# w_in in two halves behind the third v, the last unit's second layer by columns, and a new order table

## The chip, the cores and the metric

The kernel runs on one core of one Trainium2 chip. A time is device microseconds (us) of one execution, and the kernel's time is the median over executions. Each of the core's engines works off its own instructions strictly in their order: TensorE (PE) multiplies matrices, VectorE (DVE) and ScalarE (ACT) work elementwise and can read PSUM, where TensorE's results stand, GpSimd (POOL) works elementwise in SBUF, and SyncE (SP) issues DMAs. Here GpSimd issues DMAs as well, those of the weights. An instruction that waits holds up everything behind it on its engine, whatever that is.

## The reference

A gated linear attention gives x, and a two-layer network with a leaky relu is applied to x. Per batch and head, with f = sigmoid(f_logit):

```python
for t in range(S):
    state = f[:, :, t, :, None] * state + np.einsum('bhd,bhe->bhde', k[:, :, t], v[:, :, t])
    y[:, :, t] = np.einsum('bhd,bhde->bhe', q[:, :, t], state)
...
x = y.transpose(0, 2, 1, 3).reshape(B * S, H * D)
h = x @ w_in
g = np.maximum(0.01 * h, h)
out = g @ w_out
```

B = 4, H = 8, S = 768, D = 48, so x is 3072 x 384; w_in is 384 x 2048 and w_out 2048 x 384. All inputs and the output are float32.

## The kernel before, in words

The sequence is cut into 6 chunks of 128 steps. A pair j (0 to 11) is one chunk of two batches, c = j // 2 and h = j % 2; a unit (j, a) with a = 0 or 1 is one chunk of one batch, 128 rows of x. Attention goes unit by unit: a cumulative sum of log-gates by a matmul with a triangle of ones, q and k scaled with its exponentials and transposed, scores masked by the triangle, and a state of 48 x 48 per head carried from chunk to chunk. The first layer takes 16 blocks of 128 columns of w_in, the second 16 blocks of rows of w_out.

The tile framework's own scheduling is switched off. What runs when is a table of words written out by hand (`order`, L320 to L378). A loop (L379 to L381) takes word after word and records the instructions of that step, each on its engine; so the table fixes every engine's order, and semaphores fix the rest. A word is a step, the pair j, the unit a, and for some steps a third number:

- `Lf`, `Lk`, `Lq`, `Lv`: SP loads one unit's f_logit, k, q or v, 192 KB (L96 to L99); six buffers each. `st`: SP stores one unit's output (L303).
- `gate`, `dec`: ACT makes the log-gates and the exponentials. From pair 6 on, `gate`, `k`, `q` and `v` take both units in one instruction. `k`, `q`: the scaling (L155 to L165), on VectorE for k of pairs 0 to 5 and q of pairs 0 to 2, else on GpSimd. `v`: GpSimd casts v (L167 to L174).
- TensorE: `cs` (cumulative sum), `tk`, `tq` (transposes, which VectorE copies out in `ck`, `cq`), `sc` (scores, masked by VectorE in `mk`), `mx` (output of the attention, copied out by VectorE in `xt`), `pt` (state update from k and the cast v, L245 to L249; VectorE adds it in `sf`, GpSimd decays and casts the state in `sb`).
- First layer: `uu_j_a_g` (L281), four blocks of columns, 512 of w_in's 2048, for one unit, 12 matmuls, in pairs 0 to 3; `up_j_g` (L268), two blocks for both units, 6 matmuls. ACT applies the leaky relu in `pu` and `pr`. Their results stand in two PSUM buffers (`ps_m`), so a third first-layer step waits for the relu of the first.
- Second layer: `dn_j_a_quarter` (L293), four matmuls of 384 columns; four quarters make one unit, accumulated in one of two PSUM buffers (`ps_o`), which VectorE copies out in `ob` (L299).
- `W_piece_x_j_a` (L104): GpSimd issues DMAs of weights. Pieces 0 to 2 are columns of w_in (L102), three DMAs each; pieces 3 to 6 are quarters of w_out, one DMA each. The first word with a given (x, j, a) first copies one element of that unit's f, k, q or v (x = 0 to 3) to `gate_w` (L108), so the DMAs are issued only when that load has landed.
- `H_piece` (L122): SP reads four elements of that w_in piece, so what stands behind it in SP's queue is issued only when the piece has landed.

Raw loads, weight pieces and stores share the core's 16 DMA engines. SP's queue holds loads and stores in the order of the table: a store that waits for its copy holds up the loads behind it.

Of the kernel before, what the change touches and what calls it, by code (L numbers as in the profile page):

```python
# [9 lines left out]
FP32 = mybir.dt.float32  # L10
# [5 lines left out]
def kernel(  # L16
# [85 lines left out]
    w_in_cols = ((0, FF // 4), (FF // 4, FF // 2), (FF // 2, FF))  # L102
# [200 lines left out]
    def store(j, a):  # L303
        c, h = pairs[j]
        t = (2 * h + a) * S + c * C
        nc.sync.dma_start(out=out[t:t + C, :], in_=st[j].pop(("osb", a)))
# [7 lines left out]
        "up": up, "pr": relu, "uu": up_unit, "pu": relu_unit, "W": weights, "H": hold, "dn": down, "ob": out_copy, "st": store,  # L314
        "Lf": lambda j, a: load(j, "f", a), "Lk": lambda j, a: load(j, "k", a),
# [17 lines left out]
    dec_3_0 tk_2_1 uu_2_0_2 ck_2_1 pt_2_1 pu_2_0_1 k_3_0 q_3_0 sc_2_1 pu_2_0_2 Lq_3_1 uu_2_0_3 mk_2_1_1 sf_2_1
    dn_0_1_0 pu_2_0_3 mk_2_1_0 dn_0_0_0 v_3_0 tq_3_0 mx_2_1 cq_3_0 tk_3_0 xt_2_1 sb_2_1 dn_0_0_1 ck_3_0 dn_0_1_1
    sc_3_0 uu_2_1_0 mk_3_0_0 dn_0_1_2 mk_3_0_1 pu_2_1_0 Lv_3_1 dn_0_0_2 mx_3_0 Lf_4_0 uu_2_1_1 gate_3_1 xt_3_0 Lk_4_0
    dn_0_0_3 pu_2_1_1 cs_3_1 ob_0_0 uu_3_0_0 Lq_4_0 dec_3_1 uu_2_1_2 st_0_0 pu_3_0_0 dn_0_1_3 k_3_1 q_3_1 pu_2_1_2
    uu_2_1_3 Lv_4_0 ob_0_1 v_3_1 gate_4_0 tq_3_1 dn_1_0_0 st_0_1 cq_3_1 pu_2_1_3 tk_3_1 dn_1_1_0 Lf_4_1 ck_3_1
    dn_1_0_1 Lk_4_1 sc_3_1 dn_1_0_2 Lq_4_1 mk_3_1_1 v_4_0 dn_1_1_1 mk_3_1_0 Lv_4_1 uu_3_0_1 mx_3_1 Lf_5_0 pu_3_0_1
    dn_1_1_2 xt_3_1 gate_4_1 Lk_5_0 uu_3_0_2 dn_1_0_3 Lq_5_0 pu_3_0_2 pt_3_0 cs_4_0 ob_1_0 dn_1_1_3 Lv_5_0 dec_4_0
    sf_3_0 v_4_1 cs_4_1 pt_3_1 ob_1_1 st_1_0 dn_2_0_0 sb_3_0 dec_4_1 sf_3_1 dn_2_1_0 st_1_1 k_4_0 dn_2_0_1 gate_5_0  # L340
    q_4_0 k_4_1 dn_2_1_1 Lf_5_1 sb_3_1 tq_4_0 Lk_5_1 dn_2_0_2 cq_4_0 tk_4_0 q_4_1 Lq_5_1 dn_2_0_3 ck_4_0 tk_4_1 v_5_0
    Lv_5_1 ob_2_0 tq_4_1 dn_2_1_2 cq_4_1 dn_3_0_0 st_2_0 ck_4_1 gate_5_1 dn_2_1_3 Lf_6_0 sc_4_2 ob_2_1 dn_3_0_1 Lk_6_0
    mk_4_0_1 uu_3_1_0 mk_4_0_0 st_2_1 dn_3_0_2 v_5_1 mk_4_1_1 pu_3_1_0 Lq_6_0 cs_5_0 mk_4_1_0 dn_3_1_0 dec_5_0 Lv_6_0
    mx_4_2 k_5_0 q_5_0 Lf_6_1 uu_3_1_1 xt_4_0 tk_5_0 Lk_6_1 pu_3_1_1 tq_5_0 xt_4_1 cs_5_1 uu_3_0_3 ck_5_0 dec_5_1
# [67 lines left out]
```

## Time and profile before

| | us |
|---|---|
| median of 3 runs (lowest, highest) | 195.43 (194.84, 195.71) |
| the profiled execution | 195.99 |
| its span, first to last instruction | 194.2 |
| TensorE busy | 176.0, 91% of the span |
| VectorE, ScalarE, GpSimd busy | 100.2, 98.7, 77.4 |
| second layer on TensorE (L296) | 73.4, 384 matmuls |
| first layer on TensorE (L273, L286) | 52.1 and 28.0 |
| load of one unit's f, k, q or v, issue to landing (median) | 4.3 to 4.6 |
| DMA of a quarter of w_out, issue to landing (median) | 8.4 |
| store of one unit, issue to landing (median) | 3.0 |

How lines of the profile are read: the slices cut the span into 40 equal parts of 4.9 us, and a digit is the share of the slice in tenths. In a table by stage a line gives the stage in us, its length, then busy time (and count) of TensorE's matmuls, its weight loads, VectorE, ScalarE and GpSimd, the granted clock, the DMA share and GB/s. In a timeline a line has start, length, engine, source line, operation, out<-in, shape and count; the bracket is how long the engine stood idle just before and what ended that. SPq is SP's queue; the length there is how long the issue itself took. In a list of DMA issues the last number is the median from issue to landing in us.

### The profile page before, as it was taken

The page shows a single profiled execution, that of the slowest core. Times are in us where ns is not written, and L with a number is a line of the kernel's source. Part 1 is how long each engine was busy: PE and PEld are TensorE (multiplying, and loading weights), DVE is VectorE, ACT ScalarE, POOL GpSimd, SP SyncE. Part 2 cuts the span into 40 slices and gives each one's busy share as a digit, 9 for nine tenths or more (in the row PEclk, how much of TensorE's full clock was granted, in tenths as well). Part 3 has the DMA queues.
Part 4 walks back from the last instruction along what each step waited for, and adds up shares of the span by engine and source line. Part 5 has one row for each costly group of instructions (what it writes and reads, how often), then busy time and mean ns, then how long its engine had stood idle before and what let it go on. Part 6 is the DMA issues. An engine that isn't in the chain of part 4 may idle for free.

```text
span 194.2 us, 5607 instructions
## 1 busy us (share of the span) xinstructions
PE 176.0 (91%) x2344; PEld 137.9 (71%) x2344; DVE 100.2 (52%) x211; ACT 98.7 (51%) x201; POOL 77.4 (40%) x145
## 2 busy tenths in 40 slices
PE   0566499899999999999999999999999999999992
PEld 0343389888686756888877787879788797887650
DVE  2587553388544667577544677345363666212022
ACT  4454036985381823776895765376536334443100
POOL 8228733362331571359664693407602602000000
PEclk9999999999999999999999999999999999999998
DMA  6999989899999999899999999980100200111122
GB/s 120 192 187 188 198 166 188 158 180 211 187 187 209 181 228 235 165 193 194 179 201 194 189 231 185 213 157 0 46 3 2 81 3 0 44 41 44 41 81 81
DMA packets 105201, 27.10 MB, mean 140 GB/s; under 512 B 100440, under 2 KB 104280, under 8 KB 105176
## 3 DMA queue, kind: packets, MB, share of 16 engines
q1 hardware_dynamic: 103304, 23.60, 64.2%
q0 software_dynamic: 1872, 3.15, 9.2%
q8 instruction: 18, 0.29, 0.6%
q14 instruction: 7, 0.06, 0.1%
HBM read 25.17 MB, written 4.72 MB: 154 GB/s over the span
## 4 chain that ended last, share of the span: by engine, by line
PE 80%; SPq 5%; POOL 3%; ACT 3%; DMA 2%; DVE 2%; issue 1%; POOLq 0%; DVEq 0%
PE po L296 30%; PE pm L273 22%; PE pm L286 10%; SPq L98 5%; PE py L237 5%; PE tp L185 5%; PE pw L204 4%; DMA f_raw<-in_f_logit_dram 2%; PE cs L139 2%; PE pt L248 2%; POOL qh L164 1%; ACT gT L291 1%; POOL sb L261 1%; ACT em_t L149 1%; POOL sf L258 1%
## 5 line engine op out<-in xcount | busy, mean ns | idle before, releaser
L296 PE MATMUL po<-w_out_b,gT 128*128 128x384 bf16 x384 | 73.4, 326 | 0.0
L279 ACT ACTIVATE gT<-pm 128x512 bf16<-128x512 f32 x64 | 37.7, 596 | 36.0 <-PE pm L273 35.5
L273 PE MATMUL pm<-xT,w_in_b 128*128 128x256 bf16 x384 | 52.1, 273 | 0.0
L296 PEld LDWEIGHTS <-gT 128*128 128x128 bf16 x384 | 35.7, 98 | 17.7 <-issue 0.2
L273 PEld LDWEIGHTS <-w_in_b 128*128 128x128 bf16 x384 | 40.6, 114 | 4.7 <-issue 0.2
L209 DVE TENSOR_TENSOR wm<-pw,ut 128x512 bf16<-128x512 f32 x48 | 30.6, 683 | 15.0 <-PE pw L204 14.9
L291 ACT ACTIVATE gT<-pm 128x512 bf16<-128x512 f32 x32 | 18.8, 600 | 26.7 <-PE pm L286 26.5
L301 DVE COPY osb<-po 128x384 f32<-128x384 f32 x24 | 13.3, 556 | 32.5 <-PE po L296 32.2
L286 PE MATMUL pm<-xT,w_in_b 128*128 128x128 bf16 x384 | 28.0, 228 | 0.4 <-ACT gT L291 0.3
L286 PEld LDWEIGHTS <-w_in_b 128*128 128x128 bf16 x384 | 24.6, 117 | 2.4 <-issue 0.6
L243 DVE CAST xT<-py 128x384 bf16<-128x384 f32 x24 | 12.9, 554 | 14.8 <-PE py L237 14.8
L164 POOL TENSOR_TENSOR qh<-q_raw,a_t 128x384 bf16<-128x384 f32 (+1 forms) x12 | 15.7, 1310 | 11.5 <-ACT a_end L153 9.1
L171 POOL CAST v_b<-v_raw 128x384 bf16<-128x384 f32 (+1 forms) x18 | 11.6, 642 | 21.3 <-DMA v_raw<-in_v_dram 13.7
L261 POOL CAST sb<-sf 64x192 bf16<-64x192 f32 x40 | 13.6, 341 | 13.0 <-PE py L237 10.8
L258 POOL TENSOR_TENSOR sf<-sf,a_end 128x192 f32<-128x192 f32 x20 | 10.8, 538 | 18.1 <-DVE sf L254 17.9
L133 ACT ACTIVATE e_t<-f_raw 128x384 f32<-128x384 f32 (+1 forms) x18 | 11.4, 632 | 11.5 <-DMA f_raw<-in_f_logit_dram 11.4
L158 POOL TENSOR_TENSOR kh<-k_raw,em_t 128x768 bf16<-128x768 f32 x6 | 9.9, 1647 | 13.1 <-ACT em_t L149 8.8
L149 ACT ACTIVATE em_t<-cs 128x384 bf16<-128x384 f32 x24 | 11.8, 490 | 6.2 <-PE cs L142 6.1
L139 PE MATMUL cs<-lf,ut 128*128 128x384 bf16 x24 | 8.4, 351 | 6.8 <-ACT lf L134 6.7
L188 DVE COPY qT<-tp 128x512 bf16<-128x512 bf16 x24 | 10.2, 423 | 7.0 <-PE tp L185 6.8
L188 DVE COPY kT<-tp 128x512 bf16<-128x512 bf16 x24 | 9.9, 420 | 5.4 <-PE tp L185 5.3
L185 PE MATMUL tp<-ident,qh 128*128 128x128 bf16 x96 | 10.2, 234 | 2.2 <-DVE qh L164 1.8
(44 smaller groups left out, 173.2 us busy)
## 6 DMA issues: line engine op xcount, KB each, us to landing
f_raw<-in_f_logit_dram SPq DMA_DIRECT2D x24, 192.0 KB, 4.4
k_raw<-in_k_dram SPq DMA_DIRECT2D x24, 192.0 KB, 4.5
q_raw<-in_q_dram SPq DMA_DIRECT2D x24, 192.0 KB, 4.6
v_raw<-in_v_dram SPq DMA_DIRECT2D x24, 192.0 KB, 4.3
out_dram<-osb SPq DMA_DIRECT2D x24, 192.0 KB, 3.0
w_out_b<-in_moe_w_out_dram POOLq DMA_DIRECT2D x4, 384.0 KB, 8.4
w_in_b<-in_moe_w_in_dram POOLq DMA_DIRECT2D x6, 128.0 KB, 6.5
w_in_b<-in_moe_w_in_dram POOLq DMA_DIRECT2D x3, 256.0 KB, 8.5
```

What stands on the lines that cost most here:

```text
L149: nc.scalar.activation(em[:, a], t[:, 0:H * D], AF.Exp, scale=1.0)
L164: eng.tensor_mul(qhs[j % NR][:, a, :, 0:D], raw(j, "q")[:, a], st[j]["a"][:, a].rearrange("t a (h d) -> t a h d", d=D))
L185: nc.tensor.transpose(tp[:, p, :], scaled(j, x)[:, a, 2 * p:2 * p + 2, :], ident)
L188: nc.vector.tensor_copy(out=turned(j, x)[:, P2 * a:P2 * a + P2, :], in_=st[j].pop(("tp" + x, a)))
L209: nc.vector.tensor_mul(wm, st[j].pop(("pw", a, i)), ut[:, None, :].to_broadcast([128, P2, 128]))
L261: nc.gpsimd.tensor_copy(out=sb[rows, a, :, i * D:i * D + D], in_=sf[rows, a])
L273: nc.tensor.matmul(pm[:, i, :], w_in_b[:, kk, columns(ff)], st[j]["xT"][:, kk].rearrange("t a s -> t (a s)"), start=(kk == 0), stop=(kk == ...
L279: nc.scalar.activation(gT[:, 2 * g:2 * g + 2, :], st[j].pop(("pm", g)), AF.Prelu, alpha=0.01)
L286: nc.tensor.matmul(pm[:, i, :], w_in_b[:, kk, columns(ff)], st[j]["xT"][:, kk, a, :], start=(kk == 0), stop=(kk == NK - 1))
L291: nc.scalar.activation(gT[:, 4 * g:4 * g + 4, 128 * a:128 * a + 128], st[j].pop(("pu", a, g)), AF.Prelu, alpha=0.01)
L296: nc.tensor.matmul(po, st[j]["g"][:, ff, 128 * a:128 * a + 128], w_out_b[:, ff, :], start=(ff == 0), stop=(ff == NF - 1))
L301: nc.vector.tensor_copy(out=osb, in_=st[j].pop(("po", a)))
```

## The change

w_in comes in two pieces of 1024 columns (2 x 3 DMAs) in place of pieces of 512, 512 and 1024 (3 x 3 DMAs), and GpSimd issues the first when v of unit (1,0), the third unit, has landed, not its q. SP's hold is for the first piece, which covers the same columns as before. w_out is now gated on v of unit (2,0) in place of v of (2,1). The last unit's second layer is computed by columns: first 256 columns over all 16 blocks of w_out, then 128, each part with its own PSUM buffer, copy and store (`dp`, `op`, `sp`). Six late stores are made of two DMAs of 192 columns each. The order table is new throughout: k is scaled and turned ahead of q in the first units, the steps of later units stand in other places against each other, and the last units end in another order.

The diff, with the table cut to its beginning and end:

```diff
                           in_=srcs[name][2 * h + a, :, c * C:(c + 1) * C, :].rearrange("h t d -> t h d"))
 
     seen = set()
-    w_in_cols = ((0, FF // 4), (FF // 4, FF // 2), (FF // 2, FF))
+    w_in_cols = ((0, FF // 2), (FF // 2, FF))
 
     def weights(piece, x, j, a):
 
@@ -300,10 +300,33 @@
         osb = st[j]["osb", a] = opool.tile([128, KD], FP32, name="osb", tag="osb")
         nc.vector.tensor_copy(out=osb, in_=st[j].pop(("po", a)))
 
-    def store(j, a):
+    def store(j, a, parts=1):
         c, h = pairs[j]
         t = (2 * h + a) * S + c * C
-        nc.sync.dma_start(out=out[t:t + C, :], in_=st[j].pop(("osb", a)))
+        osb = st[j].pop(("osb", a))
+        for i in range(parts):
+            cols = slice(i * KD // parts, (i + 1) * KD // parts)
+            nc.sync.dma_start(out=out[t:t + C, cols], in_=osb[:, cols])
+
+
+    last_cols = (slice(0, 256), slice(256, KD))
+
+    def down_part(j, a, i):
+        cols = last_cols[i]
+        po = st[j]["pp", i] = ps_o.tile([128, KD], FP32, name="po", tag="po")
+        for ff in range(NF):
+            nc.tensor.matmul(po[:, cols], st[j]["g"][:, ff, 128 * a:128 * a + 128], w_out_b[:, ff, cols],
+                             start=(ff == 0), stop=(ff == NF - 1))
+
+    def out_part(j, a, i):
+        cols = last_cols[i]
+        osb = once(j, ("osb", a), lambda: opool.tile([128, KD], FP32, name="osb", tag="osb"))
+        nc.vector.tensor_copy(out=osb[:, cols], in_=st[j].pop(("pp", i))[:, cols])
+
+    def store_part(j, a, i):
+        c, h = pairs[j]
+        t = (2 * h + a) * S + c * C
+        nc.sync.dma_start(out=out[t:t + C, last_cols[i]], in_=st[j]["osb", a][:, last_cols[i]])
 
     parts = {
         "gate": gate, "cs": cs, "dec": dec, "k": scale_k, "q": scale_q, "v": cast_v,
@@ -312,69 +335,70 @@
         "xk": lambda j: turn_dma(j, "k"), "xq": lambda j: turn_dma(j, "q"),
         "sc": score, "mk": mask, "mx": mix, "xt": x_out, "pt": state, "sf": state_add, "sb": state_end,
         "up": up, "pr": relu, "uu": up_unit, "pu": relu_unit, "W": weights, "H": hold, "dn": down, "ob": out_copy, "st": store,
+        "dp": down_part, "op": out_part, "sp": store_part,
         "Lf": lambda j, a: load(j, "f", a), "Lk": lambda j, a: load(j, "k", a),
         "Lq": lambda j, a: load(j, "q", a), "Lv": lambda j, a: load(j, "v", a),
     }
 
 
     order = """
-    Lf_0_0 Lk_0_0 Lq_0_0 Lv_0_0 Lf_0_1 gate_0_0 Lk_0_1 cs_0_0 Lq_0_1 dec_0_0 Lv_0_1 v_0_0 q_0_0 Lf_1_0 k_0_0 gate_0_1
-    tq_0_0 Lk_1_0 pt_0_0 cq_0_0 tk_0_0 sf_0_0 Lq_1_0 cs_0_1 ck_0_0 dec_0_1 Lv_1_0 sc_0_0 v_0_1 mk_0_0_0 Lf_1_1
-    gate_1_0 k_0_1 Lk_1_1 q_0_1 pt_0_1 Lq_1_1 tk_0_1 mk_0_0_1 W_0_2_1_0 tq_0_1 sf_0_1 cs_1_0 Lv_1_1 cq_0_1 mx_0_0
-    dec_1_0 ck_0_1 W_1_2_1_0 sc_0_1 xt_0_0 gate_1_1 q_1_0 mk_0_1_1 tq_1_0 W_2_2_1_0 mk_0_1_0 cs_1_1 cq_1_0 mx_0_1
-    dec_1_1 k_1_0 sb_0_0 xt_0_1 tk_1_0 k_1_1 v_1_0 ck_1_0 tk_1_1 sb_0_1 q_1_1 pt_1_0 sc_1_0 ck_1_1 sf_1_0 tq_1_1
-    mk_1_0_0 uu_0_0_0 v_1_1 cq_1_1 mk_1_0_1 sc_1_1 pu_0_0_0 uu_0_1_0 mk_1_1_1 H_1 Lf_2_0 uu_0_0_1 mk_1_1_0 pu_0_1_0
-    Lk_2_0 mx_1_0 pu_0_0_1 Lq_2_0 uu_0_1_1 xt_1_0 sb_1_0 mx_1_1 pu_0_1_1 uu_1_0_0 xt_1_1 pt_1_1 Lv_2_0 uu_1_1_0
-    pu_1_0_0 sf_1_1 uu_1_0_1 pu_1_1_0 sb_1_1 uu_1_1_1 pu_1_0_1 Lf_2_1 gate_2_0 uu_0_1_2 Lk_2_1 pu_1_1_1 cs_2_0
-    pu_0_1_2 uu_0_0_2 Lq_2_1 dec_2_0 uu_0_1_3 Lv_2_1 v_2_0 pu_0_0_2 q_2_0 Lf_3_0 pu_0_1_3 uu_0_0_3 k_2_0 gate_2_1
-    tq_2_0 Lk_3_0 tk_2_0 cq_2_0 uu_1_1_2 ck_2_0 pu_0_0_3 Lq_3_0 cs_2_1 sc_2_0 pu_1_1_2 uu_1_1_3 mk_2_0_1 Lv_3_0
-    dec_2_1 W_3_3_2_1 pt_2_0 mk_2_0_0 uu_1_0_2 Lf_3_1 W_4_3_2_1 pu_1_1_3 sf_2_0 mx_2_0 pu_1_0_2 uu_1_0_3 W_5_3_2_1
-    q_2_1 Lk_3_1 gate_3_0 xt_2_0 tq_2_1 W_6_3_2_1 cq_2_1 uu_2_0_0 pu_1_0_3 sb_2_0 k_2_1 cs_3_0 pu_2_0_0 uu_2_0_1 v_2_1
-    dec_3_0 tk_2_1 uu_2_0_2 ck_2_1 pt_2_1 pu_2_0_1 k_3_0 q_3_0 sc_2_1 pu_2_0_2 Lq_3_1 uu_2_0_3 mk_2_1_1 sf_2_1
-    dn_0_1_0 pu_2_0_3 mk_2_1_0 dn_0_0_0 v_3_0 tq_3_0 mx_2_1 cq_3_0 tk_3_0 xt_2_1 sb_2_1 dn_0_0_1 ck_3_0 dn_0_1_1
-    sc_3_0 uu_2_1_0 mk_3_0_0 dn_0_1_2 mk_3_0_1 pu_2_1_0 Lv_3_1 dn_0_0_2 mx_3_0 Lf_4_0 uu_2_1_1 gate_3_1 xt_3_0 Lk_4_0
...
-    dn_7_1_3 dn_10_1_2 ob_7_1 up_11_6 st_7_1 dn_10_1_3 pr_11_6 up_11_7 ob_10_1 dn_11_0_0 st_10_1 pr_11_7 dn_9_0_0
-    dn_11_0_1 dn_9_0_1 dn_11_0_2 dn_9_0_2 dn_11_0_3 dn_9_0_3 ob_11_0 st_11_0 dn_11_1_0 ob_9_0 st_9_0 dn_9_1_0
-    dn_11_1_1 dn_9_1_1 dn_11_1_2 dn_9_1_2 dn_11_1_3 dn_9_1_3 ob_11_1 st_11_1 ob_9_1 st_9_1
+    Lf_0_0 Lk_0_0 Lq_0_0 Lv_0_0 Lf_0_1 gate_0_0 Lk_0_1 cs_0_0 Lq_0_1 dec_0_0 Lv_0_1 v_0_0 k_0_0 Lf_1_0 q_0_0 gate_0_1
+    tk_0_0 Lk_1_0 tq_0_0 ck_0_0 pt_0_0 cq_0_0 Lq_1_0 cs_0_1 sf_0_0 sc_0_0 dec_0_1 Lv_1_0 v_0_1 mk_0_0_1 Lf_1_1 k_0_1
+    gate_1_0 mk_0_0_0 tk_0_1 Lk_1_1 q_0_1 cs_1_0 Lq_1_1 pt_0_1 ck_0_1 dec_1_0 tq_0_1 sf_0_1 Lv_1_1 mx_0_0 W_0_3_1_0
+    cq_0_1 xt_0_0 sc_0_1 gate_1_1 k_1_0 W_1_3_1_0 mk_0_1_0 tk_1_0 mk_0_1_1 cs_1_1 ck_1_0 mx_0_1 dec_1_1 sb_0_0 q_1_0
+    xt_0_1 tq_1_0 v_1_0 k_1_1 cq_1_0 sb_0_1 tk_1_1 q_1_1 sc_1_0 ck_1_1 tq_1_1 v_1_1 mk_1_0_0 pt_1_0 mk_1_0_1 pt_1_1
+    sf_1_0 mx_1_0 cq_1_1 H_0 Lf_2_0 uu_0_0_0 sb_1_0 xt_1_0 Lk_2_0 sc_1_1 sf_1_1 pu_0_0_0 Lq_2_0 uu_0_1_0 mk_1_1_0
+    uu_1_0_0 pu_0_1_0 mk_1_1_1 pu_1_0_0 uu_1_0_1 Lv_2_0 mx_1_1 pu_1_0_1 uu_0_1_1 xt_1_1 sb_1_1 Lf_2_1 uu_0_0_1
+    pu_0_1_1 Lk_2_1 gate_2_0 uu_0_0_2 Lq_2_1 pu_0_0_1 cs_2_0 pu_0_0_2 uu_0_0_3 Lv_2_1 W_3_3_2_0 dec_2_0 uu_1_0_2
+    Lf_3_0 W_4_3_2_0 pu_0_0_3 q_2_0 W_5_3_2_0 Lk_3_0 pu_1_0_2 uu_1_0_3 k_2_0 gate_2_1 W_6_3_2_0 tq_2_0 tk_2_0 cq_2_0
+    uu_0_1_2 v_2_0 ck_2_0 pu_1_0_3 cs_2_1 sc_2_0 pu_0_1_2 pt_2_0 mk_2_0_1 uu_0_1_3 dec_2_1 mk_2_0_0 uu_1_1_0 pu_0_1_3
+    q_2_1 mx_2_0 Lq_3_0 pu_1_1_0 uu_1_1_1 k_2_1 xt_2_0 dn_0_0_0 pu_1_1_1 sf_2_0 uu_1_1_2 v_2_1 tk_2_1 pu_1_1_2
+    dn_0_1_0 ck_2_1 sb_2_0 tq_2_1 dn_0_1_1 cq_2_1 uu_1_1_3 sc_2_1 pu_1_1_3 pt_2_1 mk_2_1_1 dn_0_0_1 sf_2_1 dn_0_1_2
+    Lv_3_0 dn_0_0_2 mk_2_1_0 Lf_3_1 uu_2_0_0 gate_3_0 mx_2_1 Lk_3_1 pu_2_0_0 dn_0_0_3 xt_2_1 sb_2_1 Lq_3_1 cs_3_0
+    ob_0_0 dn_0_1_3 dec_3_0 Lv_3_1 dn_1_0_0 ob_0_1 v_3_0 uu_2_1_0 k_3_0 st_0_0 q_3_0 gate_3_1 dn_1_0_1 st_0_1 tk_3_0
+    tq_3_0 pu_2_1_0 ck_3_0 pt_3_0 cs_3_1 cq_3_0 dn_1_0_2 Lf_4_0 dec_3_1 sf_3_0 sc_3_0 Lk_4_0 dn_1_0_3 mk_3_0_1 v_3_1
+    Lq_4_0 dn_1_1_0 k_3_1 q_3_1 uu_2_1_1 ob_1_0 Lv_4_0 mk_3_0_0 tk_3_1 pu_2_1_1 tq_3_1 dn_1_1_1 st_1_0 ck_3_1 gate_4_0
...
+    up_11_3 st_9_0_2 pr_10_7 dn_9_1_0 pr_11_3 up_11_4 dn_9_1_1 pr_11_4 up_11_5 dn_9_1_2 pr_11_5 up_11_6 dn_9_1_3
+    pr_11_6 up_11_7 ob_9_1 dn_10_0_0 st_9_1_2 pr_11_7 dn_11_0_0 dn_10_0_1 dn_11_0_1 dn_10_0_2 dn_11_0_2 dn_10_0_3
+    dn_11_0_3 ob_10_0 st_10_0_2 dn_10_1_0 ob_11_0 st_11_0 dn_10_1_1 dn_10_1_2 dn_10_1_3 dp_11_1_0 ob_10_1 st_10_1
+    op_11_1_0 sp_11_1_0 dp_11_1_1 op_11_1_1 sp_11_1_1
```

## The prediction

> **What bounds the kernel now.** I read the page's slices first, then busy time by stage, then the timelines of TensorE, SP's queue and GpSimd between 22 and 53 us, and last the chain of waits and the end.
>
> ```profile
> PE 176.0 (91%) x2344; PEld 137.9 (71%) x2344; DVE 100.2 (52%) x211; ACT 98.7 (51%) x201; POOL 77.4 (40%) x145
> PE   0566499899999999999999999999999999999992
> DMA  6999989899999999899999999980100200111122
> ```
>
> TensorE is the bound from the sixth slice on; the DMA engines are as full until 130 us. By stage, TensorE idles 0.53 us between 29 and 41, 0.05 between 41 and 53, 0.43 between 70 and 73, and nothing else until 184:
>
> ```profile
> 29.00:41.00 12.00, 11.47 (x231) 10.43 (x222) 5.44 (x12) 10.06 (x23) 4.29 (x10) 1.00 0.93 168
> 41.00:53.00 12.00, 11.95 (x212) 9.06 (x200) 8.15 (x16) 6.35 (x14) 5.24 (x11) 1.00 1.04 198
> 70.00:73.00 3.00, 2.57 (x22) 1.62 (x21) 1.74 (x4) 1.04 (x2) 1.85 (x4) 1.00 1.27 208
> 130.00:184.00 54.00, 54.00 (x676) 43.31 (x675) 21.69 (x43) 24.35 (x44) 12.99 (x19) 1.00 0.08 28
> ```
>
> So a reordering has little to win after 29 us, and each new wait of TensorE costs its whole length. What can be won lies ahead of 29 us and in the tail. Two more places matter. In the timelines, TensorE waits 2.19 us for a cast behind GpSimd's DMA issues; twelve matmuls of 128 columns cost 1.37 us before 29 us and 0.76 after it, though the clock row shows full speed throughout:
>
> ```profile
> 22.64 0.48 PE L248 MATMUL pt<-v_b,kh 128*128 128x96 bf16 x4 [2.19 <-POOL v_b L171]
> 25.95 2.75 PE L286 MATMUL pm<-xT,w_in_b 128*128 128x128 bf16 x24
> 31.12 3.02 PE L286 MATMUL pm<-xT,w_in_b 128*128 128x128 bf16 x48
> ```
>
> And the w_out DMAs starve the loads beside them. SP's queue and GpSimd:
>
> ```profile
> 28.73 0.70 SPq L98 DMA_DIRECT2D v_raw<-in_v_dram  x1
> 32.26 2.34 SPq L98 DMA_DIRECT2D v_raw<-in_v_dram  x1
> 36.16 1.32 SPq L98 DMA_DIRECT2D q_raw<-in_q_dram  x1
> 37.53 0.78 SPq L98 DMA_DIRECT2D v_raw<-in_v_dram  x1
> 39.18 7.71 SPq L98 DMA_DIRECT2D k_raw<-in_k_dram  x1
> ```
> ```profile
> 37.37 0.18 POOL L108 COPY gate_w<-v_raw 1x1 f32<-1x1 f32 x1 [3.02 <-DMA v_raw<-in_v_dram]
> 37.60 2.18 POOL L116 DMA_DIRECT2D w_out_b<-in_moe_w_out_dram  x4
> 50.40 0.50 POOL L171 CAST v_b<-v_raw 128x384 bf16<-128x384 f32 x1 [4.85 <-PE pw L204]
> ```
> ```profile
> v_raw<-in_v_dram SPq DMA_DIRECT2D x1, 192.0 KB, 12.8
> ```
>
> The last line is the issue at 37.53 alone, v of unit (3,0): it landed after 12.8 us (50.3), where the median of a v load is 4.3, and SP's next issue but one stuck for 7.71. In the kernel before nothing suffers: the pt of that unit stands at 64.55.
>
> **The change part by part.** I place steps by TensorE's work: I add up the blocks ahead of a step at full-speed row durations (uu 0.67, up 0.66, dn 0.65, cs 0.27, tk or tq 0.22, sc 0.33, pt 0.17, mx 0.34, or 0.51 with a state) and look up when the kernel before had done as much. A step has "room until" that time.
>
> *Start.* Gating w_in on v of (1,0) instead of q puts its first issue from 14.50 to about 15.55 (SP issues those two loads 1.06 apart). GpSimd then issues 6 DMAs, not 9, and the ninth's 1.22 us wait goes: it is free near 18.9, not 20.7, so the two v casts of unit 1 are done near 20.8 and 22.9. pt_1_1 and mx_1_0 now precede the first uu. That uu needs the first half of w_in, for which SP's hold ended at 24.3 in the kernel before; 1.05 us later less what larger pieces save gives 23.2 to 24.8, and I take 24.5, nearest to the hold's row because the bytes are the same. As much work was done at 24.5 before: cost 0, bounds -1.1 (started at 23.4) and +0.4. The k-before-q swaps on VectorE change no matmul's place by more than its neighbour and lie under the waits for loads. From 24.5 on the second half lands by 28.7 as before, and the uu that needs it has room until 31.8.
>
> The page "TensorE: Matmul & The Clock Gate" of the Trainium skill (Part 1) says that the array runs at half rate until a free-running window of about 3.4 us has been busy. The rows bear out the half rate and a switch near 29.0, and contradict the clock row; by that rule the dense stretch, from 24.5 instead of 22.64, would switch between 27.9 and 31.3, which would make my sum -0.5 to +1.2 for this term where the rows, with the same switch, make it 0.
>
> *29 to 41 us.* ACT's order there (gate 0.98, dec 0.80, relu 0.50 to 0.60) makes TensorE wait for three uu buffers, about 0.2 + 0.3 + 0.5 by these rows, against 0.53 idle and about as much in stretched blocks before: 0, bounds -0.5 and +0.5.
>
> *w_out gated on v of (2,0).* This is the dear part. That load, issued at 28.73, lands near 32.65; gate_w and the first issue then follow as at 37.37 and 37.60, so w_out is issued from 32.9, 4.7 us earlier. The cast of that v is queued behind gate and issues (2.36 us) and ends near 35.6; its pt has room until 37.6: cost 0. The load beside it is now v of (2,1), issued 32.26 to 34.60: it stands to the w_out issue as v of (3,0) did. That one landed 12.7 us after the first w_out issue (50.34 against 37.60), so I put this one at 45.6; cast 0.50, so v_b is there at 46.2, and POOL's later steps and pt_2_1 on TensorE, with everything behind it, wait. pt_2_1 has room until 44.8: the three uu and one cs that no longer stand ahead of it (2.28) are replaced by three dn and one sc (2.28). Cost 46.2 - 44.8 = +1.4; bounds 0 (landing before 44.1) and +2.0. The dn blocks have their w_out in time: landing 6.1 to 11.3 us after issue, at 39.0 to 45.9; they have room until 40.4 to 48.4.
>
> q of (2,1), issued at 31.12 and landed 36.38 before, is 3.5 us short of landing when w_out is issued. q of (3,0) was 3.45 us short then (36.16, landed 41.05) and came through. So 0, at the very edge; the rival below prices the other side.
>
> *Units 3 to 8.* Their attention comes mostly 2 to 11 us earlier by work, so later loads have less room. Tightest: GpSimd casts v of unit 7 ahead of k_6, q_6, k_7. In the kernel before that cast starts at 93.45, with its load. 1.16 + 3 x 1.61 later k_7 would be there at 99.4, and tk_7_0 has room until 97.8. One or two stores fewer stand ahead of these loads (192 KB at some 200 GB/s, 1 us each), and the 1.4 of delay from pt_2_1 covers the rest: 0, bounds 0 and +1.4. The wait of tk_4_1 and tq_4_1 in the kernel before (0.60 around 70.5, behind POOL's q scaling of 0.92 to 1.24 and two sb) need not come back, since some 4.5 us of TensorE's work now lie between sb_3_1 and q_4_1: -0.3, bounds -0.6 and 0.
>
> *Tail.* Sixteen 256-column and sixteen 128-column matmuls (0.66/6 and 0.67/12 each) take 2.65 against 2.60: +0.05. The last copy falls from 0.56 (384 columns) to about 0.27, an estimate on the line through that row and the 0.34 of a 192-column add: -0.29. The last store moves a third of 192 KB: -0.15, bounds 0 and -0.5. The extra SP issues (0.33 each) lie beside TensorE. Together -0.4.
>
> **Sum.** The profiled execution took 195.99 (span 194.2, 1.8 around it), 0.56 above the median of 195.43. 195.99 + 0 + 0 + 1.4 - 0.3 - 0.4 = 196.7. The wait for v is set by the DMA engines, so I leave it against the profiled time; it is 1.3 (0.6%) above the median.
>
> **The rivals.**
> 1. *q of (2,1) starves too.* VectorE takes q_2_1, then k_2_1, in order, and tk_2_1 waits for it with room until 41.8. If one DMA engine's share stays behind w_out, q lands at 43 to 45.5, k_2_1 ends 1.2 later: +2.4 to +4.9 in place of 1.4, so 197.7 to 200.2. For: the 3.48 against 3.45. Against: q of (3,0) came through. The same skill page and part says that an idle window throttles the array again; at 4.9 us idle that would add up to 1.7 to this rival, and no run here shows it.
> 2. *v lands in time*, before 44.1: w_out and load share more evenly. 195.99 - 0.7 = 195.3, no change. Against: 12.8 us.
> 3. *Faster: the start is won.* The first half of w_in lands by 23.2, the first uu starts at 23.4 with 0.5 us more done: -1.1, so 195.99 - 1.1 - 0.7 = 194.2. It decides only if v of (2,1) is there by 43.1; otherwise the wait eats it.
> 4. *Loads bound unit 7*: rival 2, but tk_7_0 pays its 1.4: again 196.7; on top of a late v it adds up to 0.8, 197.5.
>
> **How the numbers follow.** About 0.5% (1 us) is what a measurement here tells from no change. Forecast (196.2 to 197.2) 0.45; rival 1 0.23; rival 2 0.14; rival 3 0.08; rival 4 0.10. Faster than 194.45: rival 3 and a corner of 2, 0.10. Within 194.45 to 196.41: most of 2 and the lower third of the forecast, 0.28. Slower: 0.62. The range leaves out rival 3 and the upper part of rival 1: 194.7 to 199.2. The forecast's own range is 196.0 to 197.4.
>
> **What would show it.** Right: w_out issued near 32.9; one v load of some 12 us; pt of (2,1) waiting for POOL's cast near 46 by about 1 to 2 us, the one large wait after 41; no idle after 130; the last copy under 0.35. Rival 1: a q load over 10 us and a tp wait near 42. Wrong at the root: the v load issued near 32 lands in under 10 us, or TensorE's first uu starts before 23.5.

## The result and the profile after

The changed kernel takes 196.68 us (median of 20 runs, 195.46 to 198.64) against 195.48 for the kernel before (20 runs, 194.21 to 197.0): ratio 1.0064, 95% interval 1.0043 to 1.0084. It is slower, by some 1.2 us. The profiled execution took 196.51 with a span of 194.7; that of before had 195.99 and 194.2, so the two traces differ by only 0.5 us: the one of before lies 0.5 above its median, this one 0.2 below.

The page of the changed kernel, busy time and slices of the span:

```profile
PE 175.8 (90%) x2360; PEld 138.5 (71%) x2360; DVE 100.7 (52%) x212; ACT 99.5 (51%) x201; POOL 76.1 (39%) x142
PE   0547599997999999999899999999999999999994
```

TensorE's busy time is that of before to 0.2 us; the loss is waiting. By stage (length, then busy time of TensorE matmul, weight load, VectorE, ScalarE, GpSimd, clock, DMA, GB/s):

```profile
29.00:41.00 12.00, 11.46 (x218) 10.25 (x217) 5.83 (x12) 10.00 (x23) 3.42 (x7) 1.00 1.05 189
41.00:53.00 12.00, 10.72 (x141) 7.95 (x140) 5.81 (x11) 5.52 (x12) 4.75 (x11) 1.00 1.06 207
70.00:73.00 3.00, 3.00 (x54) 2.56 (x52) 2.95 (x4) 2.03 (x4) 1.48 (x3) 1.00 1.22 211
73.00:100.00 27.00, 26.16 (x386) 21.29 (x384) 12.15 (x26) 18.50 (x38) 12.14 (x18) 1.00 1.05 196
```

TensorE idles 1.28 between 41 and 53 and 0.84 between 73 and 100, two holes that before did not have; the one at 70 is closed, and between 130 and 184 there is none. The first hole, on SP's queue, GpSimd and TensorE:

```profile
32.36 2.23 SPq L98 DMA_DIRECT2D v_raw<-in_v_dram  x1
35.81 5.77 SPq L98 DMA_DIRECT2D k_raw<-in_k_dram  x1
```
```profile
32.84 2.19 POOL L116 DMA_DIRECT2D w_out_b<-in_moe_w_out_dram  x4
...
45.45 0.51 POOL L171 CAST v_b<-v_raw 128x384 bf16<-128x384 f32 x1 [9.31 <-DMA v_raw<-in_v_dram]
```
```profile
44.33 0.40 PE L204 MATMUL pw<-qT,kT 48*128 48x128 bf16 x8
46.01 0.33 PE L248 MATMUL pt<-v_b,kh 128*128 128x96 bf16 x4 [1.28 <-POOL v_b L171]
```

w_out is issued at 32.84, v of (2,1) lands at 45.40, 13.0 us after its issue, and pt of (2,1) waits 1.28. The second hole, at unit 6, in the timeline of all engines:

```profile
93.11 0.83 POOL L171 CAST v_b<-v_raw 128x768 bf16<-128x768 f32 x1 [7.54 <-DMA v_raw<-in_v_dram]
...
94.24 1.64 POOL L158 TENSOR_TENSOR kh<-k_raw,em_t 128x768 bf16<-128x768 f32 x1
...
95.94 0.23 PEld L185 LDWEIGHTS <-kh 128*128 128x128 bf16 x4 [0.92 <-POOL kh L158]
95.94 0.40 PE L185 MATMUL tp<-ident,kh 128*128 128x128 bf16 x4 [0.66 <-ACT gT L279]
```

GpSimd waits for v of unit 7, casts it, and only then scales k of unit 6, whose tk TensorE is waiting for: the weight load, which reads the scaled k, names it. The matmul's own row puts the 0.66 of idle time down to a relu of ACT, which ended at the same moment (95.92, k at 95.88); that it is k which holds tk is shown by experiment 1, where k comes earlier and the wait is gone. The end:

```profile
191.55 1.09 SPq L329 DMA_DIRECT2D out_dram<-osb  x2
191.99 0.29 DVE L324 COPY osb<-po 128x128 f32<-128x128 f32 x1 [0.47 <-PE po L318]
```

The ledger of the two traces: at equal work of TensorE (blocks added up at full-speed durations, as in the prediction), how much later than before the changed kernel is.

| place (time after) | later by, us |
|---|---|
| dn_0_1_0 (42.05) | -0.2 |
| pt_2_1 (46.01) | +1.2 |
| uu_3_0_0 (69.64) | +0.8 |
| up_4_1 (78.89), past the old wait at 70 | +0.2 |
| dn_3_1_3 (92.08) | +0.2 |
| tk_7_0 (99.15) | +1.35 |
| up_6_4 (119.73) | +1.9 |
| last matmul ends (191.95) | +1.6 |
| span ends (194.7) | +0.5 |

Of the 1.4 lost at pt of (2,1) 1.0 is back by 79; 1.1 more is lost at units 6 and 7 and 0.5 up to 119, and behind the last matmul 1.1 comes back. That is not the prediction's sum, though it comes to nearly the same total. The theory on record was that the wait for v costs 1.4 for good; the rival that I took to the chip was that the loads pace TensorE anyway, and that this wait is only one place where it shows.

### The profile page after: what moved, and what is told of

Its sections match the earlier page's. It is cut to its first block, busy times and chain, and to the rows that moved or that the text cites. A ratio compares the mean times of both kernels' runs of the same rounds, so it can differ in the third digit from the quotient of the medians.

```text
span 194.7 us, 5643 instructions
## 1 busy us (share of the span) xinstructions
PE 175.8 (90%) x2360; PEld 138.5 (71%) x2360; DVE 100.7 (52%) x212; ACT 99.5 (51%) x201; POOL 76.1 (39%) x142
## 4 chain that ended last, share of the span: by engine, by line
PE 65%; DMA 13%; issue 8%; SPq 7%; POOL 5%; ACT 1%; DVE 0%; POOLq 0%
PE po L296 27%; PE pm L273 19%; SPq L98 6%; PE pm L286 5%; DMA w_in_b<-in_moe_w_in_dram 4%; DMA v_raw<-in_v_dram 4%; PE py L237 4%; DMA f_raw<-in_f_logit_dram 4%; PE tp L185 4%; PE pw L204 2%; PE po L318 1%; PE pt L248 1%; PE cs L139 1%; POOL kh L158 1%; POOL w_out_b L116 1%
## 5 line engine op out<-in xcount | busy, mean ns | idle before, releaser
L296 PE MATMUL po<-w_out_b,gT 128*128 128x384 bf16 x368 | 70.4, 326 | 0.0
L273 PE MATMUL pm<-xT,w_in_b 128*128 128x256 bf16 x384 | 50.8, 273 | 0.0
L296 PEld LDWEIGHTS <-gT 128*128 128x128 bf16 x368 | 33.6, 98 | 17.3 <-issue 0.4
L291 ACT ACTIVATE gT<-pm 128x512 bf16<-128x512 f32 x32 | 18.9, 598 | 21.0 <-PE pm L286 20.4
L301 DVE COPY osb<-po 128x384 f32<-128x384 f32 x23 | 12.8, 557 | 26.9 <-PE po L296 26.6
L171 POOL CAST v_b<-v_raw 128x384 bf16<-128x384 f32 (+1 forms) x18 | 11.1, 619 | 36.4 <-DMA v_raw<-in_v_dram 36.0
L133 ACT ACTIVATE e_t<-f_raw 128x384 f32<-128x384 f32 (+1 forms) x18 | 11.4, 633 | 13.2 <-DMA f_raw<-in_f_logit_dram 13.2
L261 POOL CAST sb<-sf 64x192 bf16<-64x192 f32 x40 | 14.3, 356 | 7.4 <-PE py L237 5.1
L185 PE MATMUL tp<-ident,kh 128*128 128x128 bf16 x96 | 10.2, 234 | 4.4 <-DVE kh L158 3.6
L253 DVE TENSOR_TENSOR sf<-sf,pt 64x192 f32<-64x192 f32 x20 | 6.9, 344 | 10.5 <-PE pt L248 9.4
```

What stands on the lines that cost most here:

```text
L185: nc.tensor.transpose(tp[:, p, :], scaled(j, x)[:, a, 2 * p:2 * p + 2, :], ident)
L261: nc.gpsimd.tensor_copy(out=sb[rows, a, :, i * D:i * D + D], in_=sf[rows, a])
L273: nc.tensor.matmul(pm[:, i, :], w_in_b[:, kk, columns(ff)], st[j]["xT"][:, kk].rearrange("t a s -> t (a s)"), start=(kk == 0), stop=(kk == ...
L291: nc.scalar.activation(gT[:, 4 * g:4 * g + 4, 128 * a:128 * a + 128], st[j].pop(("pu", a, g)), AF.Prelu, alpha=0.01)
L296: nc.tensor.matmul(po, st[j]["g"][:, ff, 128 * a:128 * a + 128], w_out_b[:, ff, :], start=(ff == 0), stop=(ff == NF - 1))
L301: nc.vector.tensor_copy(out=osb, in_=st[j].pop(("po", a)))
```

## The experiments

**1. Take each wait away (three runs beside the kernel before on one chip).** The first moves pt of (2,1) behind three dn blocks:

```diff
- sc_2_1 pu_1_1_3 pt_2_1 mk_2_1_1 dn_0_0_1 sf_2_1 dn_0_1_2 Lv_3_0 dn_0_0_2 mk_2_1_0 Lf_3_1
+ sc_2_1 pu_1_1_3 mk_2_1_1 dn_0_0_1 dn_0_1_2 Lv_3_0 dn_0_0_2 pt_2_1 mk_2_1_0 sf_2_1 Lf_3_1
```

> The changed kernel with the one pt of unit (2,1) moved behind three dn blocks (1.95 us of TensorE's work), and its sf behind the next mask; the loads, the w_out issue and GpSimd's order stay. Theory (the late v load costs its wait and nothing else): the v load still lands about 45.4 and its cast still ends about 46.0, but TensorE reaches pt at 46.5 and the 1.35 us of wait behind sc of (2,1) is gone; 195.4 (1.2 less than the changed kernel's 196.68, level with the kernel before, ratio 1.000). Rival (the loads set the pace of units 6 and 7, where k of unit 6 on GpSimd comes behind v of unit 7): TensorE comes 1.2 us earlier to tk of unit 6 and waits there up to 1.2 us longer (2.0 instead of 0.8), so 196.3 to 196.7.

The second moves the cast of v of unit 7:

```diff
- Lv_8_0 v_7_0 dec_6_1 ... k_6_0 ... q_6_0 ... tk_6_1 k_7_0 pr_5_1
+ Lv_8_0 dec_6_1 ... k_6_0 ... q_6_0 ... tk_6_1 k_7_0 v_7_0 pr_5_1
```

> The changed kernel with one word moved: the cast of v of unit 7 behind k_6, q_6 and k_7 on GpSimd, not ahead of them. Theory: k_6 starts when its em is there, at 92.4 instead of 94.24, and is done at 94.0, ahead of TensorE (95.1); the waits of 0.82 and 0.34 us at tk_6_0 and ahead of tk_7_0 go, the one at pt of (2,1) stays: 195.6 (1.1 less than the changed kernel, ratio 1.0005). Rival (the load of k of unit 6, or the pm buffers, hold TensorE there, not GpSimd's order): the waits stay, 196.7.

The third does both:

> Both of those moves together in the changed kernel. If the two waits are independent: 1.2 + 1.1 less, 194.4, ratio 0.9945 to the kernel before. If what is won at pt of (2,1) is waited for again at units 6 and 7, because the loads there do not come earlier: about 195.2 to 195.6, ratio 0.999 to 1.001.

Measured, as ratios to the kernel before: 1.0026 (0.9994 to 1.0059), 1.0069 (1.0032 to 1.0106) and 1.0041 (1.0009 to 1.0073), against 1.0064 for the changed kernel, which ran on another chip. The first is inconclusive by its time: the interval holds both forecasts. The second shows no gain where 1.1 us was expected, and the two together did not reach the kernel before, let alone 0.9945; a gain of some tenths of a microsecond over the changed kernel would be lost in these intervals. Yet the waits went: in the second run GpSimd scales k of unit 6 at 92.89 instead of 94.24, and TensorE's lateness grows by 0.25 between 92 and 100 us, not by 1.1. It is lost again later, in that run at up_6_4 (ACT, then TensorE):

```profile
117.82 0.84 ACT L133 ACTIVATE e_t<-f_raw 128x768 f32<-128x768 f32 x1 [1.86 <-DMA f_raw<-in_f_logit_dram]
118.69 0.84 ACT L134 ACTIVATE lf<-e_t 128x768 bf16<-128x768 f32 x1
119.44 1.07 ACT L279 ACTIVATE gT<-pm 128x512 bf16<-128x512 f32 x2
```
```profile
120.07 0.81 PE L273 MATMUL pm<-xT,w_in_b 128*128 128x256 bf16 x6 [0.59 <-ACT gT L279]
```

ACT waits for f of unit 10, does the gate's two passes (1.7 us), and two relus stand behind it in its queue; TensorE waits for their buffer. The same holds at unit 8, and there it is seen best in the third run: with both waits taken away TensorE does not idle between 41 us and this place, and then idles 1.42 us at once, behind f of unit 8:

```profile
98.40 0.84 ACT L133 ACTIVATE e_t<-f_raw 128x768 f32<-128x768 f32 x1 [1.72 <-DMA f_raw<-in_f_logit_dram]
```
```profile
100.66 0.82 PE L273 MATMUL pm<-xT,w_in_b 128*128 128x256 bf16 x6 [1.42 <-ACT gT L279]
```

The landing of the second f load and the block that waits for it, in us:

| run | f of (8,1) lands | up_5_4 starts | later by | f of (10,1) lands | up_6_4 starts | later by |
|---|---|---|---|---|---|---|
| changed kernel | 98.19 | 100.47 | 2.28 | 117.39 | 119.73 | 2.34 |
| pt moved | 97.77 | 100.04 | 2.27 | 117.57 | 119.91 | 2.34 |
| v of unit 7 moved | 97.83 | 100.11 | 2.28 | 117.73 | 120.07 | 2.34 |
| both moved | 98.38 | 100.66 | 2.28 | 117.92 | 120.26 | 2.34 |

Whatever was won ahead of it, TensorE comes to up_6_4 2.34 us after that load has landed. The landing does not follow TensorE in turn: from 87 us to there SP's queue never pauses for more than 0.2 us in these four profiles. The rival holds, at a place that I had not named: not k of unit 6 but f, by way of ACT's queue.

The first run's profile also shows the late load itself missing. There v of (2,1) landed at 40.46 and its cast ran at 40.51, so its pt had nothing to wait for; the load that came late was f of (3,0), 13.07 us after the first w_out issue, with k, q and v of (3,0) behind it, and tq of that unit idled 0.53 for its q, which GpSimd scales behind the cast of that v. Its executions may therefore be of both kinds, and its median does not say what the starved v alone is worth.

**2. Take the pins away.** The gates of units 8, 10 and 11 go behind later relus:

```diff
- gate_8_0 tq_6_0 ... pr_5_3 up_5_4
+ tq_6_0 ... pr_5_3 gate_8_0 up_5_4
- gate_10_0 sc_7_2 ... pr_6_3 Lq_11_0
+ sc_7_2 ... pr_6_3 gate_10_0 Lq_11_0
- gate_11_0 mx_8_2 ... pr_8_6 up_8_7
+ mx_8_2 ... pr_8_6 gate_11_0 up_8_7
```

> The changed kernel with three words moved: the gates (ACT's two passes over f) of units 8, 10 and 11 stand behind pr_5_3, pr_6_3 and pr_8_6, so that a late load of f no longer holds up relus of the second layer's blocks. Theory P (the landings of f pin TensorE: in the changed kernel and in the three runs made from it, up_5_4 starts 2.28 us after f of (8,1) lands and up_6_4 2.34 us after f of (10,1), whatever came before): both intervals cease to hold, but the waits at pt of (2,1) and at units 6 and 7 stay, so only 0.2 to 0.4 us is won: 0.998 of the changed kernel. Rival (those waits were independent of the loads): 0.

> The three gates moved, and pt of (2,1) and v of unit 7 moved as well: the two moves that together brought nothing. Theory P: without the pins the gains add up to what TensorE had lost, 1.2 to 2.0 us less than the changed kernel run beside it (ratio to the kernel before 0.996 to 1.000), and TensorE reaches up_6_4 by 118.6, not 119.7 to 120.3. Rival (the loads pin it at a further place, k or q of units 7 to 9): no more than 0.5 less.

The changed kernel ran beside them:

> The changed kernel itself, to be compared with the others on the same chip: ratio to the kernel before 1.0064 again (1.004 to 1.009); in its profile up_5_4 starts 2.28 after f of (8,1) lands and up_6_4 2.34 after f of (10,1), and v of (2,1) lands 44.5 to 46.5.

On this chip the changed kernel has 196.01 us (1.0058, 1.0031 to 1.0085), the gates alone 195.97 (1.0051, 1.0025 to 1.0077), and gates and both words 194.52 (0.9982, 0.9960 to 1.0004): 1.5 us less than the changed kernel beside it. The three gates by themselves brought 0.04, which fits the rival's 0 and does not exclude the 0.2 to 0.4 of theory P; the two words by themselves (on the other chip) left it 0.4% behind before. In the version with all five moves TensorE does not idle between 41 and 184, and it reaches up_6_4 at 117.99, 2.10 after the landing:

```profile
41.00:53.00 12.00, 12.00 (x165) 8.98 (x157) 6.87 (x14) 6.13 (x13) 4.74 (x11) 1.00 1.11 210
73.00:100.00 27.00, 27.00 (x397) 22.38 (x395) 12.67 (x28) 19.46 (x40) 13.51 (x20) 1.00 1.03 199
```

The waits stand one behind the other, and each hides the next: the 1.42 us of the run with both words are gone, and only all the moves together give a gain that the times can tell. The repeat of the changed kernel kept 2.35 at up_6_4 (118.99 after a landing at 116.64), but missed my 2.28 at unit 8 (2.44: other waits came last there). With the gates alone I expected both intervals to cease; they are 2.50 and 2.38. The second lies close to 2.34 by chance, for there TensorE idles for nothing between 103 and 184, so an interval alone does not show a pin; ACT's own wait for f together with it does. Which of the gates and words are needed was not tried singly.

**3. The tail alone, in the kernel before.**

```diff
- dn_11_1_0 ob_9_0 st_9_0 dn_9_1_0 dn_11_1_1 dn_9_1_1 ... dn_11_1_3 dn_9_1_3 ob_11_1 st_11_1 ob_9_1 st_9_1
+ dn_11_1_0 ob_9_0 st_9_0 dn_11_1_1 dn_11_1_2 dn_11_1_3 dp_9_1_0 ob_11_1 st_11_1 op_9_1_0 sp_9_1_0 dp_9_1_1 op_9_1_1 sp_9_1_1
```

> The kernel before with only the new tail: the last unit and the unit beside it no longer alternate, and the last one's second layer goes in 256 and 128 columns, with its own copies and stores. The prediction's term is -0.4 us (195.1, ratio 0.998). The two profiled executions differ by 1.07 us between TensorE's last matmul and the end of the span (3.8 before, 2.75 after), with 0.2 more on TensorE: if that is the tail's doing, -0.9 (194.6, ratio 0.9955) and the end lies 2.7 to 2.8 after the last matmul; if it is scatter of the store, -0.3 or less and about 3.3.

0.9946 (0.9920 to 0.9972), which is 1.06 us (the medians are 196.6 and 195.45). From the last matmul to the end of the span it is 3.2 us, against 3.8 before and 2.8 in the changed kernel; the expected 2.7 to 2.8 was not met. So 0.7 is in the tail's steps; the other 0.4 of the changed kernel's 1.05 is in the last section.

In the profile of this run TensorE came 1.01 us later at unit 8, behind f of (8,1). Its gate moved as well:

> The kernel before with the new tail (ratio 0.9946 as measured) and the gate of unit 8 behind pr_5_5. Theory P: the kernel before is pinned there too, in some executions (the tail's run waited 1.01 us behind dn_4_0_3, and up_5_6 started 2.35 us after f of (8,1) landed; in the profiled execution of before the load came 0.96 earlier and nothing waited), so the mean gain is 0.2 to 0.6: ratio 0.991 to 0.994. Rival (that wait was a rare disturbance): 0.9946 again.

0.9962 (0.9938 to 0.9985): no gain that these runs can tell from the tail alone. A wait of 1 us in every execution would have shown, unless a later one takes it back, so that wait does not look regular in the kernel before.

**4. w_out early, in the kernel before.** Only the four w_out DMAs and their gating change place:

```diff
- W_3_3_2_1 ... W_4_3_2_1 ... W_5_3_2_1 ... W_6_3_2_1
+ W_3_3_2_0 W_4_3_2_0 W_5_3_2_0 W_6_3_2_0 v_2_0
```

> The kernel before with one thing of the change: w_out issued behind v of (2,0), ahead of the cast of that v, 4.7 us earlier (about 32.9 instead of 37.60). The prediction's term by itself: v of (2,1) starves and lands near 45.6, its cast ends near 46.2, pt of (2,1) waits 1.2 us (it stood at 44.83), so +1.2 us, ratio 1.006. Theory P (TensorE is held by the landings of f further on, with 0.2 us to spare at unit 8 in the profiled execution): the wait at pt is there, but half or more of it is not in the end, 1.000 to 1.004. If the load does not starve: 1.000 with no wait at pt.

203.06 us against 195.25, ratio 1.0396 (1.0356 to 1.0436): all three forecasts missed. v of (2,1) came through (39.20); the late load was f of (3,0), at 46.92 instead of 38.68, and the old order asks for it at 41.8 here (ACT, then TensorE, then a stage behind them):

```profile
46.95 0.52 ACT L133 ACTIVATE e_t<-f_raw 128x384 f32<-128x384 f32 x1 [6.78 <-DMA f_raw<-in_f_logit_dram]
```
```profile
48.08 0.48 PE L139 MATMUL cs<-lf,ut 128*128 128x384 bf16 x1 [6.11 <-ACT lf L134]
```

```profile
48.00:50.00 2.00, 1.92 (x19) 1.75 (x19) 0.00 (x0) 1.82 (x6) 0.16 (x1) 0.50 1.01 189
```

The wait is not all of it. The granted clock (third number from the end) is 0.50 behind it: by the trace it fell at 46.72, 4.75 us after TensorE had gone idle, and came back at 53.54, and in between matmuls of 128 columns take 107 ns again. Against the kernel before TensorE is 1.2 us ahead at 41, 5.1 behind at 48.1 and 7.5 behind at 53.7, so some 6.3 us are the wait and 2.5 the clock.

So early w_out costs 7.8 us with the old order, where the new one, which comes to cs of unit 3 at 50.1 instead of 43.0, stalls 1.3 at pt of (2,1). The edit's parts cannot be priced apart from one another.

**5. What starves the load.** The changed kernel with w_out in packets of 384 bytes:

```diff
- nc.gpsimd.dma_start(out=w_out_b[:, part * n:(part + 1) * n, :], in_=moe_w_out[...])
+ for lo in (0, KD // 2):
+     cols = slice(lo, lo + KD // 2)
+     nc.gpsimd.dma_start(out=w_out_b[:, part * n:(part + 1) * n, cols], in_=moe_w_out[..., cols])
```

> The changed kernel with each of the four w_out DMAs split into two of 192 columns, so that a packet writes 384 bytes instead of 3072 (estimate from the rows of w_in and w_out packets, 97 ns at 1024 bytes, 173 at 2048 and 247 at 3072: some 50 ns each). Theory of turns (a DMA engine serves its queues packet by packet in turn, and a load's small packets wait behind one large one each time): v of (2,1) now waits 50 ns a turn instead of 247 and lands by 37 to 41, not 45.4; the last w_out DMA lands at 47 to 52 instead of 44.6, so the pt of (2,1) no longer waits but a dn may, by up to 3 us. Rival (the load is simply held until w_out's bytes are through): v lands with the last of w_out again, at 45 or later. Time 195 to 199 us; what tells them apart is the landing.

v of (2,1) was handed over 1.4 us after the first w_out issue and yet landed at 40.03, in 6.1 us; f, k and q of (3,0) followed at 42.7, 46.7 and 49.7, the last of w_out at 50.83. The engines serve the two queues in turn, packet by packet; from 42 to 48 us, with loads and w_out in flight, the trace has as many packets of the one queue (q0, GpSimd's) as of the other (q1, SP's):

```profile
q0 software_dynamic: 1763, 0.66, 87.8%
q1 hardware_dynamic: 1761, 0.33, 50.7%
```

The Trainium skill says so in "DMA: Bandwidth & Descriptors", section "Queues, rings and completion order" (each engine switches between queues at packet boundaries), and this trace agrees.

A load of 192 KB is 1024 packets of 192 bytes, and a quarter of w_out here 1024 packets of 384: v, f, k and q landed one beside each quarter, which landed at 39.6, 43.7, 47.2 and 50.8. In the changed kernel all of w_out is 512 packets of 3072 bytes, of some 250 ns each, so turns let only about half a load through while it lasts; from 35 to 43 us its trace has 534 packets of the one and 489 of the other (not evenly: from 37 to 39, 147 and 19). The time is worse, 1.012 (1.0074 to 1.0167), for another reason: eight issues hold GpSimd, and the cast of v of (2,0) behind them, to 39.3, where it was 35.0, and pt of (2,0) idles 1.79 for it:

```profile
33.37 5.96 POOL L118 DMA_DIRECT2D w_out_b<-in_moe_w_out_dram  x8
39.33 0.52 POOL L173 CAST v_b<-v_raw 128x384 bf16<-128x384 f32 x1
```

**6. The start.** In the profiles of the changed kernel and its variants, with the same code up to 28 us, TensorE's matmuls of 128 columns go from 107 to 56 ns at 28.4 to 29.1 in some and only at 31.0 to 32.1 in three; there TensorE is 0.9 to 1.8 us later at cs of unit 2 (34.2 to 34.6 against 32.8 to 33.3). To the version of experiment 2 that is level with before I added 29 matmuls whose result nobody reads (the code is abridged):

```diff
+    def warm(n):
...
+        for i in range(n):
+            nc.tensor.matmul(warm_po["t"][:, 0:128], ident, ut, start=True, stop=True)
...
+ warm_4 tk_1_0 ... warm_7 tk_1_1 ... warm_14 pt_1_1 ... warm_4 uu_0_0_0
```

> The version with both words and the three gates moved, and 29 more matmuls of 128 columns whose result nobody reads, put where TensorE waits between 16 and 25 us. TensorE's matmuls changed from 107 to 56 ns a column block at 28.3 to 29.1 in some profiles of the changed kernel and its variants and at 31.0 to 32.1 in the others. If the change of rate follows how long the array has been busy, it comes by 22 to 26, and TensorE reaches cs of unit 2 one to two us earlier (31.5 to 32.5 without other waits). On the total: if nothing pins TensorE behind that, 0.5 to 1.5 us less than the version without (ratio to the kernel before 0.990 to 0.996, against 0.998); if the loads of unit 2 (f of (2,0) lands near 30) or v of (2,1) (45 to 46) take it back, 0.998 again. Rival for the rate (it changes at a set time after the start): 28.3 to 32 as before.

```profile
21.75 1.15 PE L337 MATMUL po<-ut,ident 128*128 128x128 bf16 x14
23.55 0.33 PE L248 MATMUL pt<-v_b,kh 128*128 128x96 bf16 x4 [0.65 <-POOL v_b L171]
```

Fourteen matmuls took 1.15: the fifth of them, at 22.17, is the first at the higher rate, 3.2 us after the extra matmuls beside unit 1 began at 18.98. cs of unit 2 comes at 31.31. So the rate follows the work, and not a set time after the start. The page "TensorE: Matmul & The Clock Gate" of the Trainium skill (Part 1) says so too, with a window of about 3.4 us. The 3.2 us here, and the 4.3 in the last run below (from 19.17 to about 23.5), are of that size; where the stretch is taken to begin is my choice. The total is 0.9970 (0.9948 to 0.9993) against 0.9982 without. Most of the gain is waited for again: TensorE idles 0.21 us at pt of (2,0), 0.52 at tq of (3,0) and 0.48 in three later places, where the version without does not idle. To the kernel before with the new tail and the gate of unit 8 moved I added 21 such matmuls:

> The kernel before with the new tail and the gate of unit 8 moved back (the version that had 0.9962), and 21 extra matmuls that nobody reads, where TensorE waits between 19 and 22 us. By the run with 29 of them the matmuls change to 56 ns a column block within 3 us of continuous work: here by 22 to 23.5, instead of 27.1 to 29.0, and cs of unit 2 comes 0.7 to 1.5 us earlier than in the version without (33.1). Total: 0.4 to 1.0 us less (ratio to the kernel before 0.990 to 0.994) if TensorE keeps it as far as the landing of f of (8,1); 0.995 to 0.9965 if the loads take it back.

0.9927 (0.9901 to 0.9952), 194.47 against 195.77: the lowest ratio here, below both kernels. The version without had 0.9962, so the gain looks kept (0.7 us), though the two intervals overlap.

## Why the prediction was right, and where it was not

The time (196.7 against 196.68) and the sign were right. Most of the steps around w_out were too, but the sum held by luck: a missing cost at units 6 to 10 and undersized gains at 70 us and in the tail are about equal. The premise that "each new wait of TensorE costs its whole length" did not hold.

- *Start, 0.* First issue 15.46 (15.55 forecast), GpSimd free at 18.84 (18.9), first uu at 24.45 (24.5), v casts done at 21.4 and 23.4 (20.8 and 22.9). Inside the first uu TensorE still waited 0.47 for w_in. Lateness at uu_1_0_0: 0.03. In the profiled execution the 0 holds. The bound of +0.4 was too narrow: the upper end by the clock rule, +1.2, is about what three of the later profiles show (0.9 to 1.8 at cs of unit 2). Little of it reaches the end, because pt of (2,1) then waits less (0.2 instead of 1.35 in the run with the gates alone).
- *29 to 41 us, 0.* Busy 11.46 against 11.47. Right.
- *w_out gated on v of (2,0), +1.4.* Issue 32.84 (32.9), landing 45.40 (45.6), wait 1.28, block longer by 1.35. Right in the mechanism and the local size. Two things were not. Which load starves is a matter of tenths of a microsecond. And 1.4 is not its price in the end: the pins at units 6, 8 and 10 stand behind it, and what it is worth without them was seen only together with theirs (1.5).
- *Rival 1, q of (2,1)*, did not happen in any profile; it landed at 35.9 to 37.0 throughout. What its last sentence could not show, a clock that falls again in an idle stretch, experiment 4 shows: 0.50 granted from 4.75 us of idle time on, some 2.5 us of cost.
- *Units 3 to 8, 0.* This is the step that failed. I had the cast of v of unit 7 ahead of k_6, q_6 and k_7, and k_7 done at 99.4 (it was 99.09), and then wrote that "the 1.4 of delay from pt_2_1 covers the rest". It did not: 0.6 of that delay had been won back at 70 and 0.4 before, so TensorE arrived with 0.2 and waited, first for k of unit 6 (0.82), then 0.34 more; lateness rose by 1.1 up to tk_7_0 and by 0.5 more up to up_6_4, only some 0.15 of it right at the blocks behind the gates of units 8 and 10: in this kernel those pins hardly bite, they come out when the earlier waits go. I looked for loads that come late on GpSimd and not for ACT's queue, where a gate that waits for f stands ahead of relus. This is rival 4 on top of a late v (197.5), which I had in the text with 0.10 for the whole rival.
- *The wait at 70, -0.3.* It went whole: -0.6, the lower bound.
- *Tail, -0.4.* -1.05 after the last matmul. The copy is right (end 0.33 after the last matmul, 0.60 before: -0.27). SP passes its wait for the last store 1.54 us after the issue (64 KB), against 1.90 (192 KB): -0.35 where I put -0.15. The other 0.43 I had not seen at all.

Together: 1.6 us missing at units 6 to 10, less 0.7 in the tail and 0.3 at 70, less some 0.4 drifting back between 46 and 70 and 0.3 after 120; that leaves the profiled pair 0.5 apart where I had 0.7. Why the medians are 1.2 apart and the profiles 0.5 stays open; single executions scatter by more than that. What holds for the medians is the undoing: the tail is worth 1.06 in the kernel before, and the waits that the five words move 1.5 together, on one chip each.

## What to carry to other kernels

When transfers are as full as the busiest engine, price a wait only after asking which landing that engine will wait for next: a wait ahead of a later pin costs little here, and removing it gained little, until the later pins went too. Look for pins in every in-order queue, above all where an engine that feeds the bottleneck (here the relus) also does the first step on a fresh load. And small transfers handed over beside large-packet ones should be those with the most time to spare; that order was not tried here.

## What the runs showed of the hardware that I had not expected

- Which load starves is decided by its hand-over. With w_out in 3072-byte packets: where SP's issue ended 0.06 to 0.21 us after the start of the first w_out issue, the load landed 3.5 to 6.3 us after that start (five profiles); the first load whose issue ended 0.58 to 1.95 after, 12.2 to 13.2 us (all thirteen), and the next two or three behind it within 3 us more. So it is not one load that starves, but all that are handed over after w_out. The starts of the issues do not separate the two: -0.49 came through in one profile and starved in another. A blocked issue also takes longer, so the end is partly a consequence.
- The rate of the matmuls changes some 3 us apart for the same code (28.4 to 32.1 with the changed start, 26.1 to 29.1 with the old one), while the clock row shows 1.00 throughout. The traces' first record of the granted clock stands at that very change (28.98 before, 29.01 in the changed kernel, 22.17 and 23.52 with the extra matmuls), so the row's 1.00 ahead of it is no reading; at 0.50, in experiment 4, it is one.
- The end of the program depends on more than the last store. In the kernel before and in the tail's run, 1.2 to 1.3 us pass from SP's passing its wait for that store (192.90, 192.98) to the end, because SP steps through seven (six) further waits of 0.06 each behind it; in the changed kernel these had been passed earlier, and from 193.85 it is 0.9. That was 0.4 us, by nothing that the edit meant to do.
